# First token half of a fused attention and gated expert kernel in plain fp32 from unsplit weights

## The chip, the cores and the metric

One core of a Trainium2 chip runs the kernel. Its engines run side by side, each through its own queue in order: PE multiplies matrices, DVE (vector), ACT (scalar, with activation tables) and POOL work on tiles in the on-chip memory, and SP issues the transfers (DMA). The metric is the device time of one execution in microseconds (us), as a median over several executions.

## The reference

The attention looks at a window of 31 keys around each query and at one summary per block of 32 keys (the maximum of the keys, the mean of the values). Its output goes, heads side by side, into a gated expert layer in which each token is mixed with the one before it.

```python
scores_l = scale * np.matmul(q, k.transpose(0, 1, 3, 2))      # q, k, v: 4 x 8 x 768 x 64
scores_s = scale * np.einsum('bhsd,bhnd->bhsn', q, k_sum)
scores_s = scores_s + np.log(block)
scores_l_m = np.where(mask_l, scores_l, -1000000000.0)
scores_all = np.concatenate([scores_l_m, scores_s], axis=-1)
a = np.exp(scores_all - np.max(scores_all, axis=-1, keepdims=True))
a = a / (np.sum(a, axis=-1, keepdims=True) + 1e-09)
x = np.matmul(a, np.concatenate([v, v_sum], axis=2))
...
xk = mu_k * x + (1.0 - mu_k) * x_prev                         # 4 x 768 x 512
xr = mu_r * x + (1.0 - mu_r) * x_prev
k = np.maximum(xk @ w_k, 0.0)                                 # w_k 512 x 1024
v = k * k @ w_v                                               # w_v 1024 x 512
r = 1.0 / (1.0 + np.exp(-(xr @ w_r)))                         # w_r 512 x 512
return r * v
```

The queries, keys and values are fp32; the three weights arrive as fp64 and are turned into fp32 on the chip.

## The kernel before

**Units.** A batch has 8 heads in 4 pairs and 768 tokens in two halves of 384. A unit (`unit`) is one pair of heads for one half: on PE the scores (tile `sc`, 12 small matmuls), on DVE six masks with a row minimum (L439), on ACT six exponentials (L443), on DVE one inverse of the sums (L449, L450), on POOL six normalisations (L455), on PE six transposes (L462), on ACT two copies (L466), on PE the values (tile `av`, 12 small matmuls, L475), and a copy of the result into `vx` as features by tokens. `load_set` loads a pair's keys (`kt`) and value windows (two `vx`), makes the key maxima on DVE, and for batch 0 makes the value means on PE (L367, L387), which DVE or POOL spread into the windows (L393).

**Token halves.** The expert layer runs for eight halves, here n = 0 to 7 (n = 2 x batch + half). `mixes` makes the mixed tokens of four pairs: ACT or POOL scales (L498, L501), DVE adds (L504), ACT rounds to a high part (L507), DVE subtracts for a low part (L509). The parts have the type fp32r; each product of two numbers is made as high x high, high x low and low x high. The gate is 3 token tiles of 4 x 3 products of 512 columns (L521 to L523). `experts` then runs over 8 slices j of the hidden size: `first` (e1 in the texts, L542) has 12 products of 384 columns, then relu and square on ACT and a split into `kh` and `kl`; `second` (e2, L563) has 9 products of 512 columns. At the end DVE multiplies by the gate (L585) and SP stores.

**Weights.** There are 20 tiles of 128 x 512 (4 of w_r, 8 each of w_k and w_v). Each is loaded as 64-bit words into one of three slots `st`; ACT or POOL scales (L287, L290), DVE takes bits three times (L294, L297, L301) to give an fp32 tile, ACT or POOL rounds it to the high part (L309, L311) and DVE subtracts for the low part (L313). High and low parts of all 20 tiles have places of their own until the end.

**The order.** The code states operations with their costs and due times; `Plan.schedule` keeps a clock for each engine, takes for each engine the operation that can start first (then the one due first), hands out buffers from small pools, and writes the instructions in that order. The hardware keeps this order on each engine; what it waits for there is its own matter. At the start, matmuls on the identity (L618, "warm") fill PE until the first gate is issued. Before the change the order of the statements is: weights, all eight units of batch 0, gate of n = 0, gate of n = 1 between the slices of n = 0, and from there on each half's gate and experts with the next batch's units between.

```python
                    late = start > now
                    key = (start if late else now, o.due, o.n)
...
                for w, s in ((wk_h, 0), (wk_h, 1), (wk_l, 0)):
                    for p in range(NPAIR):
                        nc.tensor.matmul(ps.t[:, 0:HT], w[:, j, p, :], x[p][s].t, start=(n == 0), stop=(n == 11))
```

## Time and profile before

| what | value |
|---|---|
| median of 3 runs (475.34 to 480.13 us) | 479.1 us |
| span of the profiled execution | 476.2 us |
| median run less profiled span | 2.9 us |
| mean granted PE clock | 0.991 |
| memory traffic | 42.49 MB read, 6.29 MB written |
| DMA share of hardware queue | 36.0% of 16 engines' span |

No time of the profiled execution is recorded beside its span, and one of the three runs (475.34 us) is below that span, so executions differ by about that much.

In the page a row of a timeline reads: start, length, engine, line and operation, tile written and tiles read, shape, count, and in brackets how long the engine was idle before it and what ended that. The length of a row reaches past the start of the next row of its engine, so the cost of one instruction in a stream is the distance from its start to the next start. A matmul in plain fp32 leaves two records, so the 12 matmuls of a unit's scores or values show as x24. In the table by stretches, each engine has its busy time in the stretch and the number of instructions, then the granted PE clock, the busy share of the DMA engines and their GB/s.

### The profile page before, as it was taken

Reading aid. Unit: us, or ns where it says so; the run is one execution under the profiler, and the core shown is the slowest. Engines: PE = TensorE matmul, PEld = TensorE weight load, DVE = VectorE, ACT = ScalarE, POOL = GpSimd, SP = SyncE. Lnnn points to the kernel's source line nnn. Section 1 sums busy time; section 2 is a strip of 40 time slices with the busy share of each in tenths; the row PEclk is TensorE's granted clock in tenths of the full one; section 3 lists DMA queues with packets and bytes.
Section 4 is the critical chain, followed back from the end, with each engine's and each line's share of the span. In section 5 each row is a group of like instructions: output and inputs, shape, how many; then the busy total and the mean of one; then the engine's idle time right before and its main releaser. Section 6 shows DMA issues by size and latency. Waiting matters only on the chain.

```text
span 476.2 us, 9814 instructions
## 1 busy us (share of the span) xinstructions
PE 450.8 (95%) x3588; PEld 380.2 (80%) x3588; DVE 278.9 (59%) x881; ACT 285.9 (60%) x808; POOL 120.6 (25%) x255
## 2 busy tenths in 40 slices
PE   2899898879999999999999999999999999999996
PEld 2677776669888888987788888997778888888995
DVE  4699799979855386438364566429354554223223
ACT  3689675585777575428796756428886655231321
POOL 0579812230444301202342200203342201000000
PEclk9999999979999999999999999999999999999999
DMA  8991347885600209706300209907100010001001
GB/s 260 289 300 59 89 137 232 279 238 176 204 18 14 61 1 280 217 0 207 104 9 14 78 7 274 234 0 236 50 8 9 13 41 28 0 1 66 0 1 66
DMA packets 27014, 51.17 MB, mean 107 GB/s; under 512 B 2903, under 2 KB 14807, under 8 KB 26967
## 3 DMA queue, kind: packets, MB, share of 16 engines
q1 hardware_dynamic: 26967, 50.56, 36.0%
q8 instruction: 28, 0.46, 0.4%
q14 instruction: 19, 0.16, 0.1%
HBM read 42.49 MB, written 6.29 MB: 102 GB/s over the span
## 4 chain that ended last, share of the span: by engine, by line
PE 71%; ACT 8%; DVE 5%; POOL 3%; issue 2%; DVEq 0%; ACTq 0%; POOLq 0%
PE mm L563 26%; PE mm L542 25%; PE av L475 4%; PE pt L462 4%; PE mm L521 3%; PE mm L523 3%; PE mm L522 3%; PE sc L428 3%; POOL y L455 3%; ACT y L443 2%; ACT L443 2%; DVE we L297 1%; DVE xa L504 1%; DVE wc L301 1%; ACT xa L498 1%
## 5 line engine op out<-in xcount | busy, mean ns | idle before, releaser
L455 POOL TENSOR_SCALAR y<-y,rc 128x120 f32<-128x120 f32 x192 | 86.2, 467 | 164.2 <-DVE rc L450 140.1
L542 PE MATMUL mm<-xs,wk_h 128*128 128x384 f32 x512 | 102.3, 342 | 4.7 <-ACT z L527 4.1
L542 PEld LDWEIGHTS mm<-xs,wk_h 128*128 128x128 f32 x512 | 91.5, 190 | 11.0 <-ACT z L527 4.3
L547 ACT ACTIVATE r<-mm 128x384 f32<-128x384 f32 x64 | 31.3, 488 | 95.2 <-PE mm L542 95.0
L443 ACT ACTIVATE y<-y,mn 128x120 f32<-128x120 f32 x192 | 73.6, 386 | 11.1 <-DVE mn L439 10.1
L563 PE MATMUL mm<-wv_h,kh 128*128 128x512 f32 x192 | 78.7, 410 | 0.0
L563 PE MATMUL mm<-wv_l,kh 128*128 128x512 f32 x192 | 75.8, 395 | 0.0
L551 DVE CAST kh<-r 128x384 fp32r<-128x384 f32 x45 | 17.0, 378 | 73.8 <-ACT r L549 73.7
L563 PE MATMUL mm<-wv_h,kl 128*128 128x512 f32 x192 | 59.7, 406 | 0.0
L439 DVE CUSTOM_DVE_ANT_0 y<-sc,mask_sb 128x120 f32<-128x120 f32 x192 | 43.0, 276 | 24.6 <-PE sc L428 18.7
L542 PE MATMUL mm<-xs,wk_l 128*128 128x384 f32 x256 | 56.5, 343 | 0.0
L509 DVE TENSOR_TENSOR xs<-xa,xs 128x384 fp32r<-128x384 f32 x64 | 36.2, 575 | 25.1 <-ACT xs L507 25.0
L542 PEld LDWEIGHTS mm<-xs,wk_l 128*128 128x128 f32 x256 | 46.7, 192 | 0.0
L504 DVE SCALAR_TENSOR_TENSOR xa<-vx,mu_sb,xa 128x384 f32<-128x384 f32 x64 | 40.1, 646 | 6.4 <-ACT xa L498 3.8
L563 PEld LDWEIGHTS mm<-wv_h,kh 128*128 128x128 f32 x192 | 36.3, 189 | 7.1 <-issue 0.3
L553 DVE TENSOR_TENSOR kl<-r,kh 128x384 fp32r<-128x384 f32 x64 | 36.6, 571 | 7.9 <-ACT kh L552 5.1
L466 ACT COPY pts<-pt 120x384 f32<-120x384 f32 x64 | 30.4, 475 | 17.9 <-PE pt L462 17.5
L563 PEld LDWEIGHTS mm<-wv_l,kh 128*128 128x128 f32 x192 | 36.3, 189 | 5.8
L521 PE MATMUL mm<-wr_h,xs 128*128 128x512 f32 x96 | 38.8, 404 | 1.4 <-ACT r L547 1.3
L563 PEld LDWEIGHTS mm<-wv_h,kl 128*128 128x128 f32 x192 | 34.3, 188 | 6.9 <-DVE kl L553 0.2
L523 PE MATMUL mm<-wr_h,xs 128*128 128x512 f32 x96 | 38.4, 400 | 1.5 <-DVE xs L509 1.4
L462 PE MATMUL pt<-ident_sb,y 128*120 128x128 f32 x192 | 35.4, 288 | 3.6 <-POOL y L455 3.1
(63 smaller groups left out, 650.5 us busy)
## 6 DMA issues: line engine op xcount, KB each, us to landing
vx<-in_v SPq DMA_DIRECT2D x32, 360.0 KB
kt<-in_k SPq DMA_DIRECT2D x15, 544.0 KB
qt<-in_q SPq DMA_DIRECT2D x32, 192.0 KB
out<-z SPq DMA_DIRECT2D x24, 256.0 KB
st<-in_vT SPq DMA_DIRECT2D x12, 384.0 KB
st<-in_w_k SPq DMA_DIRECT2D x8, 512.0 KB
st<-in_w_v SPq DMA_DIRECT2D x8, 512.0 KB
st<-in_w_r SPq DMA_DIRECT2D x4, 512.0 KB
```

The lines of the kernel that those rows point to most:

```text
L439: op("DVE", "mask", None, lambda h=h, i=i, var=var: nc.vector.tensor_tensor_reduce(out=y[h].t[:, i, :], in0=sc[h].t[:, i, 0:NK], in1=mask_ ...
L443: op("ACT", "exp", None, lambda h=h, i=i: nc.scalar.activation(y[h].t[:, i, :], y[h].t[:, i, :], AF.Exp, bias=mn[h].t[:, i:i + 1], scale=-1.0,
L455: op("POOL", "norm", None, lambda h=h, i=i: nc.gpsimd.tensor_scalar(out=y[h].t[:, i, :], in0=y[h].t[:, i, :], scalar1=rc.t[:, NSL * h + i: ...
L462: nc.tensor.transpose(out=pt[h].t[0:NK, i * P:(i + 1) * P], in_=y[h].t[:, i, :], identity=ident_sb)
L504: op("DVE", "mixd", None, lambda xt=xt, xa=xa, p=p: nc.vector.scalar_tensor_tensor(out=xa.t, in0=xt.t[:, 1 + lo:1 + lo + HT], scalar=mu_sb ...
L509: op("DVE", "sub", None, lambda xa=xa, xh=xh, xl=xl: nc.vector.tensor_tensor(out=xl.t, in0=xa.t, in1=xh.t.bitcast(F32), op=ALU.subtract), ...
L521: nc.tensor.matmul(ps.t, xh.t[:, ts], wr_h[:, p, :], start=(p == 0), stop=False)
L523: nc.tensor.matmul(ps.t, xl.t[:, ts], wr_h[:, p, :], start=False, stop=(p == NPAIR - 1))
L542: nc.tensor.matmul(ps.t[:, 0:HT], w[:, j, p, :], x[p][s].t, start=(n == 0), stop=(n == 11))
L547: op("ACT", "relu", None, lambda: nc.scalar.activation(r.t, ps.t[:, 0:HT], AF.Relu), reads=[(ps, 0)], writes=[(r, 0)])
L553: op("DVE", "sub", None, lambda: nc.vector.tensor_tensor(out=kl.t, in0=r.t, in1=kh.t.bitcast(F32), op=ALU.subtract), reads=[(r, 0), (kh, 0 ...
L563: nc.tensor.matmul(acc[t].t, a.t[:, t * P:(t + 1) * P], w[:, j, :], start=start, stop=stop)
```

## The change

It does the following.

- The half n = 0 is computed in plain fp32. Its mixed tokens are not split (`mix` returns one tile), its gate has 12 matmuls of 512 columns (`gate_parts`), e1 has 4 matmuls of 384 columns per slice and e2 has 3 of 512, and the squared hidden tile `r` is used as it is. They read the fp32 weights before any split.
- The gate of n = 0 runs by pairs of heads: for each pair three matmuls, one for each token tile, as soon as that pair's tokens are mixed. Three accumulators stay open meanwhile.
- Only the four units of the first half of batch 0 stand ahead of n = 0; the other four are stated behind it with their own due times. A fourth `kt` place is needed for that; later it serves as two `z` tiles.
- `weight` ends with the fp32 tile. The split of all 20 tiles is a function of its own (`split`), stated behind n = 0. Fp32 tiles, high and low parts take their places from a common pool `w` of 40 slots, given back after the last use, instead of fixed places.
- The gate of n = 1 no longer stands between the slices of n = 0.
- The scheduler counts POOL's operations and those of DVE named in `LOCKS` as users of one port, one after the other; buffers can be taken out of turn; the planned DMA rate, due times and spacings are other numbers.

```diff
+GATE0 = 34000
+FULL = 34000
+STEP0 = 6800
+GATE1 = 92000
-GATES = (36000, 46000)
-WR = 0, 6000
+LOCKS = {"wbits", "wor", "wsub", "mixd", "sub", "kcopy", "khv", "spread"}
...
+                    if e == "POOL" and o.name != "tiny" or e == "DVE" and o.name in LOCKS:
+                        start = max(start, port)
...
-            if o.name == "gate" and spare:
+            if o.name == "gate32" and spare:
...
+    last_kt = Slot(const, "kt3", [P, KL], "kt3")
+    last_z = Slot(const, "z4", [P, 2, DM], "kt3")
     pools = dict(
+        ktx=[last_kt], w=slots("w", 2 * (NCK + 2 * NCV), [P, 512]),
...
-        z=tiles("z", 6, [P, DM]), xa=tiles("xa", 4, [P, HT]),
+        z=tiles("z", 4, [P, DM]), xa=tiles("xa", 4, [P, HT]),
...
-    def weight(name, i, src, dst_h, dst_l, due=None):
+    def weight(name, i, src, last, due=None):
         st, we, wc = buf("st"), buf("we"), buf("wc")
+        wf = w_f[name, i] = buf("wc") if last else buf("w", F32, False)
...
+    def split(name, i):
+        wf = w_f[name, i]
+        wh, wl = w_h[name, i], w_l[name, i] = buf("w", F32R, False), buf("w", F32R, False)
+        op("ACT", "wcast", None, lambda: nc.scalar.copy(out=wh.t, in_=value()), reads=[(wf, 0)], writes=[(wh, 0)],
...
+        op("DVE", "wsub", None, lambda: nc.vector.tensor_tensor(
+            out=wl.t, in0=value(), in1=wh.t.bitcast(F32), op=ALU.subtract), reads=[(wf, 0), (wh, 0)], writes=[(wl, 0)])
...
+    def mix(b, hf, which, p):
+        first = b + hf == 0
+        xt, xa = xts[b, p], buf("xs") if first else buf("xa")
...
+        if first:
+            return xa
...
+    def gate_parts(x, z):
+        ps = [buf("mm") for _ in range(NTT)]
+        for p in range(NPAIR):
+            for t in range(NTT):
+                op("PE", "gate32", GATE0 - (NPAIR - 1 - p) * FIRST + 930 * t, lambda p=p, t=t: nc.tensor.matmul(
+                    ps[t].t, x[p].t[:, t * P:(t + 1) * P], w_f["wr", p].t, start=(p == 0), stop=(p == NPAIR - 1)),
...
+                h, l = (w_f["wk", j], None) if single else (w_h["wk", j], w_l["wk", j])
+                terms = [(h, 0)] if single else [(h, 0), (h, 1), (l, 0)]
...
+                op("PE", "e2_32" if single else "e2a", due, high, reads=[(kh, 0), *w], writes=[(a, 0) for a in acc])
...
     for p in range(NPAIR):
-        e = load_set(0, p)
-        for h in range(2):
-            unit(0, p, h, e, GATES[0] - 2000 - (7 - 2 * p - h) * FIRST)
+        sets.append(load_set(0, p))
+        unit(0, p, 0, sets[p], GATE0 - 4000 - (NPAIR - 1 - p) * FIRST)
+        gates.append(mix(0, 0, 1, p))
+    z = [buf("z") for _ in range(NTT)]
+    gate_parts(gates, z)
+    x = mixes(0, 0, 0)
+    for p in range(NPAIR):
+        unit(0, p, 1, sets[p], gate_due(0, 1) - 9000 - (NPAIR - 1 - p) * SECOND)
+    experts(0, 0, x, z)
+    for i in range(NCK):
+        split("wr", i)
+    for j in range(NCV):
+        split("wk", j)
+        split("wv", j)
```

What the scheduler made of it is read from the order of the instructions. On PE, where the first gate stands, the order before has four last warm matmuls behind the values of the eighth unit, and then the gate's products by token tile; `wr_h`, `wr_l` are the parts of w_r, and `xs` the parts of the mixed tokens.

```order
L618 MATMUL mm_150<-ident_sb 128x128 x4
L521 MATMUL mm_153<-wr_h,xs_118 128x512
L522 MATMUL mm_153<-wr_l,xs_118 128x512
L523 MATMUL mm_153<-wr_h,xs_119 128x512
L521 MATMUL mm_153<-wr_h,xs_120 128x512
L522 MATMUL mm_153<-wr_l,xs_120 128x512
L523 MATMUL mm_153<-wr_h,xs_121 128x512
```

The same place on PE after the change shows the second and third pair's gate matmuls (L580, `w` is an fp32 tile of w_r) among a value mean (L425) and the transposes of the last pair's unit (L500).

```order
L580 MATMUL mm_135<-w_0_449,xs_0_416 128x512
L425 MATMUL mm_132<-sp_90,sel_sb 24x128
L580 MATMUL mm_133<-w_0_449,xs_0_416 128x512
L580 MATMUL mm_134<-w_0_449,xs_0_416 128x512
L580 MATMUL mm_135<-w_0_495,xs_0_489 128x512
L500 MATMUL pt_130<-ident_sb,y_93 120x128 x3
L580 MATMUL mm_133<-w_0_495,xs_0_489 128x512
L500 MATMUL pt_130<-ident_sb,y_94 120x128 x3
```

Gate matmuls of early pairs have moved ahead of the later pairs' transposes and values, and there are 15 warm matmuls in all where there were 56.

On DVE, ahead of the first gate, the order before mixes and splits the tokens (`xa` is mixed, `xs` its low part) between weights.

```order
L294 TENSOR_SCALAR we_143<-st_140 128x512
L504 SCALAR_TENSOR_TENSOR xa_117<-vx_79,mu_sb,xa_117 128x384
L504 SCALAR_TENSOR_TENSOR xa_114<-vx_70,mu_sb,xa_114 128x384
L504 SCALAR_TENSOR_TENSOR xa_115<-vx_73,mu_sb,xa_115 128x384
L509 TENSOR_TENSOR xs_125<-xa_117,xs_124 128x384
L504 SCALAR_TENSOR_TENSOR xa_116<-vx_76,mu_sb,xa_116 128x384
L509 TENSOR_TENSOR xs_127<-xa_114,xs_126 128x384
```

After the change DVE has at that place, ahead of the first e1, the last bits and splits of w_r (L328, L332, and L352 for the subtraction), those of the first tile of w_k, and then five mixes in a row, the last of the gate and the four for e1.

```order
L352 TENSOR_TENSOR w_0_516<-w_0_495,w_0_500 128x512
L328 SCALAR_TENSOR_TENSOR we_125<-st_122,we_125 128x512
L332 SCALAR_TENSOR_TENSOR w_0_524<-wc_127,we_125 128x512
L325 TENSOR_SCALAR we_125<-st_123 128x512
L328 SCALAR_TENSOR_TENSOR we_125<-st_123,we_125 128x512
L352 TENSOR_TENSOR w_0_559<-w_0_524,w_0_529 128x512
L332 SCALAR_TENSOR_TENSOR w_0_563<-wc_126,we_125 128x512
L541 SCALAR_TENSOR_TENSOR xs_0_561<-vx_79,mu_sb,xs_0_561 128x384
L541 SCALAR_TENSOR_TENSOR xs_0_565<-vx_70,mu_sb,xs_0_565 128x384
L541 SCALAR_TENSOR_TENSOR xs_0_567<-vx_73,mu_sb,xs_0_567 128x384
```

The subtractions of the tokens are gone there; those of the weights still stand among the bits. Of the 20 weight splits, the scheduler puts 4 subtractions on DVE ahead of the first e1, 12 between it and the last token split that the gate of n = 1 needs, and 4 behind.

More of the change, by code (lines that the diff above doesn't have):

```diff
@@ L185, in schedule @@
                 engines[e] = start + o.cost
+                if e == "POOL" and o.name != "tiny" or e == "DVE" and o.name in LOCKS:
+                    port = start + o.cost
                 o.finish = start + o.cost + TAIL[e]
@@ L199, in schedule @@
                         if not x.left:
[L200 removed]
+                            free_slots[x.pool].append((start, x.place))
                 spare = []
@@ L233, in tile_kernel @@
     )
-    plan = Plan(pools)
+    plan = Plan(pools, dict(ktx=("z", [Slot(const, "z", None, part=(last_z, n)) for n in range(2)])))
     op, buf = plan.op, plan.buf
@@ L241, in tile_kernel @@
     om_sb = const.tile([P, 2, NPAIR], F32, name="om_sb")
-    wk_h = const.tile([P, NCV, NCK, P], F32R, name="wk_h")
-    wk_l = const.tile([P, NCV, NCK, P], F32R, name="wk_l")
-    wv_h = const.tile([P, NCV, DM], F32R, name="wv_h")
-    wv_l = const.tile([P, NCV, DM], F32R, name="wv_l")
-    wr_h = const.tile([P, NCK, DM], F32R, name="wr_h")
-    wr_l = const.tile([P, NCK, DM], F32R, name="wr_l")
     pool_sb = const.tile([NK, 36], F32, name="pool_sb")
@@ L515, in gate_tile, with sigmoid @@
+    def mixes(b, hf, which):
+        return [mix(b, hf, which, p) for p in range(NPAIR)]
+    def sigmoid(ps, z):
+        op("ACT", "sigmoid", None, lambda: nc.scalar.activation(z.t, ps.t, AF.Sigmoid), reads=[(ps, 0)], writes=[(z, 0)])
     def gate_tile(b, hf, x, z, t):
@@ L525, in gate_tile @@
+                nc.tensor.matmul(ps.t, xl.t[:, ts], h, start=False, stop=(p == NPAIR - 1))
         op("PE", "gate", gate_due(b, hf) + 2800 * t, products, reads=[(a, 0) for pair in x for a in pair]
-           + [(("wr", i), s) for i in range(NCK) for s in "hl"], writes=[(ps, 0)])
-        op("ACT", "sigmoid", None, lambda: nc.scalar.activation(z[t].t, ps.t, AF.Sigmoid),
-           reads=[(ps, 0)], writes=[(z[t], 0)])
-    def experts(b, hf, x, z, between):
+           + [(w["wr", i], 0) for i in range(NCK) for w in (w_h, w_l)], writes=[(ps, 0)])
@@ L579, in last @@
                 def last(t=t):
[L580 to L584 removed]
+                    if single:
+                        product(t, kh, w_f, stop=True)
+                    else:
+                        product(t, kh, w_h)
+                        product(t, kh, w_l)
+                        product(t, kl, w_h, stop=True)
+                op("PE", "e2l_32" if single else "e2", due + 700 * t, last,
+                   reads=[(kh, 0), *([] if single else [(kl, 0)]), *w], writes=[(acc[t], 0)])
                 op("DVE", "result", due + 4000 + 700 * t, lambda t=t: nc.vector.tensor_tensor(
@@ L593, in experts @@
         for j in range(1, NCV + 1):
-            for work in between.get(j, ()):
-                work()
             if j < NCV:
@@ L600, in experts @@
             second(j - 1)
-    def places(name, i):
-        if name == "wr":
-            return wr_h[:, i, :], wr_l[:, i, :]
-        if name == "wv":
-            return wv_h[:, i, :], wv_l[:, i, :]
-        return [w[:, i].rearrange("p c n -> p (c n)") for w in (wk_h, wk_l)]
     for i in range(NCK):
-        weight("wr", i, w_r[i * P:(i + 1) * P, :], *places("wr", i), due=WR[0] + WR[1] * i)
+        weight("wr", i, w_r[i * P:(i + 1) * P, :], False)
     for j in range(NCV):
-        weight("wk", j, w_k[:, j * P:(j + 1) * P].rearrange("(c p) n -> p c n", p=P), *places("wk", j))
-        weight("wv", j, w_v[j * P:(j + 1) * P, :], *places("wv", j))
-    spare = buf("mm")
+        weight("wk", j, w_k[:, j * P:(j + 1) * P].rearrange("(c p) n -> p c n", p=P), False)
+        weight("wv", j, w_v[j * P:(j + 1) * P, :], j == NCV - 1)
+    spare = buf("mm", F32, False)
     for _ in range(WARM):
@@ L642, in tile_kernel @@
                     unit(b + 1, p, h, e, gate_due(b + 1, 0) - 14000 - (7 - 2 * p - h) * UNITS)
+        x, z = mixes(b, hf, 1), [buf("z") for _ in range(NTT)]
+        for t in range(NTT):
+            gate_tile(b, hf, x, z, t)
+        experts(b, hf, mixes(b, hf, 0), z)
     order = plan.schedule()
```

187 lines of the change are left out of this document (100 added, 87 removed).

## The prediction

> **What bounds the kernel now.** I read the page's head first, then the busy time by stretches, then PE's timeline and DVE's over the first 175 us.
>
> ```profile
> span 476.2 us, 9814 instructions
> PE 450.8 (95%) x3588; PEld 380.2 (80%) x3588; DVE 278.9 (59%) x881; ACT 285.9 (60%) x808; POOL 120.6 (25%) x255
> ```
>
> By this PE is the bound everywhere. The stretches (us; busy PE, PEld, DVE, ACT, POOL; granted clock; DMA share; GB/s) say otherwise for the first fifth.
>
> ```profile
> 20.00:30.00 10.00, 10.00 (x181) 7.99 (x180) 8.95 (x36) 8.61 (x35) 6.14 (x11) 1.00 1.02 263
> 40.00:50.00 10.00, 8.31 (x114) 6.72 (x113) 8.92 (x33) 7.99 (x33) 10.00 (x17) 1.00 0.27 69
> 60.00:70.00 10.00, 9.67 (x44) 7.59 (x42) 8.89 (x17) 7.58 (x14) 0.99 (x1) 1.00 0.36 118
> 80.00:90.00 10.00, 9.81 (x65) 7.81 (x64) 9.96 (x20) 5.65 (x10) 1.83 (x2) 1.00 0.81 263
> 100.00:120.00 20.00, 19.41 (x96) 17.03 (x99) 17.65 (x38) 12.64 (x30) 3.59 (x9) 0.86 0.57 174
> 200.00:300.00 100.00, 99.35 (x817) 84.18 (x816) 55.58 (x194) 66.56 (x191) 19.74 (x48) 1.00 0.32 89
> ```
>
> From 200 us on PE is full and DVE at 56%. Up to 90 us it is DVE that is full at about 90%. PE's timeline shows how little its busy time is worth there.
>
> ```profile
> 38.85 0.52 PE L462 MATMUL pt<-ident_sb,y 128*120 128x128 f32 x3
> 39.20 1.50 PE L618 MATMUL mm<-ident_sb 128*128 128x128 f32 x12
> ...
> 58.22 0.48 PE L521 MATMUL mm<-wr_h,xs 128*128 128x512 f32 x1
> 58.53 0.39 PE L522 MATMUL mm<-wr_l,xs 128*128 128x512 f32 x1
> 58.76 0.40 PE L523 MATMUL mm<-wr_h,xs 128*128 128x512 f32 x1
> 59.00 0.39 PE L521 MATMUL mm<-wr_h,xs 128*128 128x512 f32 x1
> ...
> 97.55 1.77 PE L542 MATMUL mm<-xs,wk_h 128*128 128x384 f32 x8 [3.88 <-ACT z L527]
> ...
> 173.75 0.40 PE L521 MATMUL mm<-wr_h,xs 128*128 128x512 f32 x1
> ```
>
> The first gate starts only at 58.22. The gate of n = 2 starts at 173.75, and 302.4 us follow to the end of the span; behind that gate both orders hold the same matmuls (216 of the gate, 576 of e1, 441 of e2, 16 units). So the change is worth what it does to these 173.75 us. The chain of waits gives prices where PE runs full.
>
> ```profile
> 111.93 2.08 PE mm L542 x12
> 114.01 2.09 PE mm L563 x9
> ...
> 123.41 0.78 PE sc L428 x24
> 124.19 0.85 PE av L475 x24
> ```
>
> **PE's work, added and moved.** A split product of 512 columns costs 0.2325 (59.00 less 58.53, halved), one of 384 costs 0.174 (2.08/12). For plain fp32 the warm row is the price: 12 records are 6 matmuls of 128 columns, with 0.11 between records, so 0.22 per 128 columns and 0.88 to 0.93 per 512; I take 0.93, four times 0.2325, and 0.70 for 384. Gate: 12 x 0.93 for 36 x 0.2325, +2.8. e1: 32 x 0.70 for 96 x 0.174, +5.7. e2: 24 x 0.93 for 72 x 0.2325, +5.6. Together +14.1 us of PE on n = 0 (at 0.88 it is +11.5). Forty-one fewer warm matmuls take off 9.0 us that were fillers, worth nothing where PE waits.
>
> Summed with these prices over the order after (0.78 a unit's scores, 0.85 its values, 0.34 three transposes), PE has 28.0 us ahead of the first e1, 53.5 from there to the gate of n = 1, and 58.2 from there to the gate of n = 2. Before, the 290.7 us behind the gate of n = 2 took 298.7 up to the last matmul, a pace of 1.027; so 53.5 and 58.2 take 54.9 and 59.8 if PE never waits.
>
> **DVE's work, removed and kept.** Spacings come from these rows.
>
> ```profile
> 19.29 0.55 DVE L393 COPY vx<-vm 24x768 f32<-24x768 f32 x1 [0.35 <-ACT vm L389]
> ...
> 20.08 0.28 DVE L439 CUSTOM_DVE_ANT_0 y<-sc,mask_sb 128x120 f32<-128x120 f32 x1
> ...
> 20.28 0.28 DVE L439 CUSTOM_DVE_ANT_0 y<-sc,mask_sb 128x120 f32<-128x120 f32 x1
> ...
> 41.10 1.35 DVE L504 SCALAR_TENSOR_TENSOR xa<-vx,mu_sb,xa 128x384 f32<-128x384 f32 x2
> ...
> 58.02 0.55 DVE L509 TENSOR_TENSOR xs<-xa,xs 128x384 fp32r<-128x384 f32 x1
> 58.49 0.61 DVE L504 SCALAR_TENSOR_TENSOR xa<-vx,mu_sb,xa 128x384 f32<-128x384 f32 x1
> 59.02 0.54 DVE L509 TENSOR_TENSOR xs<-xa,xs 128x384 fp32r<-128x384 f32 x1
> ...
> 62.01 0.55 DVE L509 TENSOR_TENSOR xs<-xa,xs 128x384 fp32r<-128x384 f32 x1
> ...
> 65.80 0.69 DVE L313 TENSOR_TENSOR wv_l<-wc,wv_h 128x512 fp32r<-128x512 f32 x1
> 66.40 0.85 DVE L294 TENSOR_SCALAR we<-st 128x512 uint32<-128x512 uint32 x1
> ...
> 69.28 0.43 DVE L294 TENSOR_SCALAR we<-st 128x512 uint32<-128x512 uint32 x1
> 69.62 0.55 DVE L509 TENSOR_TENSOR xs<-xa,xs 128x384 fp32r<-128x384 f32 x1
> 70.09 0.68 DVE L297 SCALAR_TENSOR_TENSOR we<-st,we 128x512 uint32<-128x512 uint32 x1
> 70.69 0.55 DVE L509 TENSOR_TENSOR xs<-xa,xs 128x384 fp32r<-128x384 f32 x1
> ...
> 75.20 0.54 DVE L553 TENSOR_TENSOR kl<-r,kh 128x384 fp32r<-128x384 f32 x1
> ...
> 90.61 0.54 DVE L553 TENSOR_TENSOR kl<-r,kh 128x384 fp32r<-128x384 f32 x1
> ...
> L585 DVE TENSOR_TENSOR z<-mm,z x24: 684/691/693, 122.4 to 472.5; 128x512 f32<-128x512 f32 x24
> ```
>
> A mask is 0.20, a mix 0.53, a token split 0.47, a weight's first bits 0.34, each later bit step 0.61, its split 0.60, a spread 0.55. The change removes 8 token subtractions, 8 of the hidden tile and its copies, some 8 to 10 us. It removes no weight work: by the order, 16 of 20 splits still stand on DVE ahead of the gate of n = 1. What it does is let PE begin n = 0 sooner.
>
> *To the first e1.* From the first spread (19.29 before; the bytes ahead of it and ahead of the last value window are the same in both orders, so I leave it) DVE has 22.2 us by these spacings to the last mix for e1: 9 masks, 6 spreads, 15 weight steps, 4 splits, 8 mixes, small rest. Before, from that spread to the mix at 41.10 stood 18.5 us of work in 21.8, a pace of 0.85. So 22.2/0.85 = 26.1, and the first e1 at 45.4 us. In PE's queue the last gate matmuls end there too: 28.0 us of work, of which some 15 lie behind the first gate matmul.
>
> *To the gate of n = 1.* DVE has 50.0 us between the last mix and the last token split: 36 masks (7.2), 42 weight steps (21.9), 12 splits (7.2), 10 mixes and token splits (5.1), small rest (8.6). Almost the same list stood before between 62.01 and the first result at 122.4: 50.8 us in 59.9 (from 62.48), pace 0.85. So 50.0/0.85 = 59.0, more than PE's 54.9: DVE decides, and the gate of n = 1 starts at 104.4.
>
> *To the gate of n = 2.* DVE has 30.3 us there, PE 59.8: PE decides, 164.2. Before it was 173.75.
>
> The gate by pairs adds a wait: PE's queue holds the third pair's gate matmuls ahead of the last pair's transposes, so a late mix of the third pair delays the last unit, and the three open accumulators leave one `mm` tile for the value means. Between nothing and the length of one pair's gate matmuls (3 x 0.93), I take nothing, since DVE, not PE, brings the last mix.
>
> ```profile
> L443 ACT ACT_TABLE_LOAD x9 | 11.5, 1283 | 0.9 <-PEq L726 0.7
> ```
>
> Costed at nothing, too: 4 more table loads on ACT (4 x 1.28 = 5.1 us) and 13 mixes that POOL did; ACT has room (5.65 to 8.61 of 10 in the stretches above), and without it those 5 us are due. SP's queue: the last w_v tile is its load 58, with 21 MB up to it, 81 us at the 263 GB/s of the stretch in which the DMA share is 1.02, while DVE gets to it after 100 us; if weights came late instead, DVE would wait, not SP. The fourth `kt` place becomes `z` after the last unit's scores, ahead of any use. The 40 shared slots: a split waits if its place's last reader is a late e1 (0 to 2 us, hidden by DVE's other work). The scheduler's port only spaces instructions.
>
> The sum: 164.2 + 302.4 = 466.6 us of span against 476.2, and with the 2.9 us of median over span, 469.5 us.
>
> **A rule against it.** POOL's normalisations slow down beside DVE.
>
> ```profile
> 50.53 4.50 POOL L455 TENSOR_SCALAR y<-y,rc 128x120 f32<-128x120 f32 x6
> ...
> 124.74 2.06 POOL L455 TENSOR_SCALAR y<-y,rc 128x120 f32<-128x120 f32 x6 [16.99 <-DVE rc L450]
> ```
>
> Six take 2.06 with a quiet DVE and 4.50 beside weight steps, so 2.44 us were lost; had all POOL work to be added to DVE's, the middle part would grow by up to 16.2 us, as the first rival works out. The Trainium skill (SBUF — State Buffer, section "SBUF: two separate sides") says that a DVE instruction with two inputs in the on-chip memory and a POOL instruction that reads there take one lock for their whole length, and that the later one waits until it is free. By that rule the time would be the 476.7 of the first rival; the trace agrees as far as the loss of 2.44 us goes.
>
> **The rivals.** *Full lock, no gain (0.22).* Between the first e1 and the gate of n = 1, POOL has 36 normalisations (36 x 0.343) and about 4 us of copies, 16.2 in all. If none of it overlaps DVE and DVE has no other idle time, the middle part is 66.2, the gate of n = 2 at 171.4, and the time 476.7. Against it: 15 of DVE's 50 us are masks and reductions, and the pace of 0.85 holds some blocking already.
>
> *The pace of the crowded start lasts, slower (0.11).* From 41.10 to 58.02 DVE did 11.6 us of work in 16.9, 0.69, since it waited for units that waited for POOL, which was busy 10.00 of 10.00. Half 1's units now stand among n = 0's slices. At 0.69 the whole 72.2 us of DVE take 104.6, the gate of n = 2 comes at 183.7, and the time is 489. The point that decides is 72.2/(173.75 - 59.8 - 19.3) = 0.76: below this pace the kernel is slower than before. An idle stretch of PE as at 97.55 (3.88 us, then the clock at 0.86 over 100 to 120) costs some 3 us more, and the warm matmuls that fill such gaps now end at the first gate.
>
> *PE bound from the first e1 on (0.17).* DVE at 0.94 (14.5 us of work between 75.20 and 90.61): 42.9 + 54.9 + 59.8 gives 157.6 and a time of 462.9.
>
> *Forecast (0.50).* The pace of 0.85 and 469.5 us.
>
> **How the numbers follow.** A median of this kernel can tell about 1% (4.8 us) from no change. Faster by over 1% means under 474.3, a pace over 0.80: the forecast and the PE-bound rival, 0.67. Within 1%: the lock rival, 0.22. Slower: 0.11. The range goes from 461 (PE-bound, with fp32 at 0.88 instead of 0.93) to 483 (pace 0.73), which leaves out most of the slow rival and a little below.
>
> **What would show it.** First e1 (L601 after) near 45 us; gate of n = 1 (L567) near 104; gate of n = 2 near 164, and the same 302 us behind it; fp32 records of 512 columns 0.46 apart; DVE near 90% busy from 25 to 100 us. It is wrong if PE waits for the hidden tile or the values rather than for DVE's weights, if normalisations take over 0.7 us throughout, or if the part behind the gate of n = 2 changes.

## The result and the profile after

The changed kernel takes 473.87 us (median of 4 runs, 471.08 to 475.29) against 477.92 us before (475.34 to 480.13): a ratio of 0.990 with a 95% interval from 0.9858 to 0.9943. The forecast was 469.5 us, its range 461 to 483. The sign was right and the range held; of the 9.6 us that the sum took off the span the medians show 4.05, under half. That is less than the 1% (4.8 us) that counted as measurable, though the interval does not reach 1; the median lies under the 474.3 us named there only because the kernel before was at 477.92 this time, not 479.1. The profiled execution of the changed kernel had a span of 473.5 us and a time of 475.29, so 1.8 us lie around a span. The 2.9 us that the forecast added were partly the difference between two executions.

The head of the page, then the stretches that were read before the change, with the one from 50 to 60 us added (us, busy PE, PEld, DVE, ACT, POOL, granted clock, DMA share, GB/s):

```profile
span 473.5 us, 9475 instructions
PE 447.6 (95%) x3438; PEld 357.9 (76%) x3438; DVE 267.0 (56%) x865; ACT 292.6 (62%) x815; POOL 112.5 (24%) x236
```

```profile
20.00:30.00 10.00, 10.00 (x161) 8.33 (x161) 7.86 (x33) 7.09 (x25) 4.03 (x9) 1.00 1.00 246
40.00:50.00 10.00, 8.53 (x69) 4.57 (x67) 9.79 (x28) 8.59 (x14) 0.84 (x1) 1.00 0.40 126
50.00:60.00 10.00, 6.56 (x57) 4.09 (x57) 5.94 (x27) 9.90 (x30) 4.83 (x8) 0.75 0.45 134
60.00:70.00 10.00, 10.00 (x50) 5.34 (x49) 8.78 (x24) 8.43 (x28) 8.03 (x12) 0.91 0.58 195
80.00:90.00 10.00, 10.00 (x98) 5.93 (x97) 9.96 (x41) 8.80 (x34) 3.86 (x7) 1.00 1.03 307
100.00:120.00 20.00, 17.41 (x139) 11.96 (x134) 17.68 (x54) 16.80 (x43) 7.93 (x15) 1.00 0.69 183
200.00:300.00 100.00, 99.27 (x814) 83.69 (x813) 54.77 (x193) 68.60 (x196) 23.02 (x52) 1.00 0.33 97
```

DVE is at 9.79 of 10 from 40 to 50 us and at 9.96 from 80 to 90, near the forecast's 90% and more. Between, from 50 to 60 us, lies a hole: DVE is at 5.94 there and ACT at 9.90: an engine that the forecast had called roomy is full there. PE's timeline shows the places that the forecast named.

```profile
44.77 2.84 PE L580 MATMUL mm<-w,xs 128*128 128x512 f32 x6 [1.47 <-DVE xs L541]
47.45 2.74 PE L601 MATMUL mm<-xs,w 128*128 128x384 f32 x8
50.12 0.84 PE L466 MATMUL sc<-kt,qt 64*64 64x120 f32 x24
53.95 0.33 PE L500 MATMUL pt<-ident_sb,y 128*120 128x128 f32 x1 [2.98 <-POOL y L493]
...
57.10 5.17 PE L601 MATMUL mm<-xs,w 128*128 128x384 f32 x8
...
109.34 0.50 PE L567 MATMUL mm<-w,xs 128*128 128x512 f32 x1 [0.79 <-ACT r L608]
...
124.72 0.52 PE L500 MATMUL pt<-ident_sb,y 128*120 128x128 f32 x3 [1.68 <-POOL y L493]
...
171.94 0.39 PE L567 MATMUL mm<-w,xs 128*128 128x512 f32 x1
```

Four fp32 matmuls of 384 columns take 50.12 - 47.45 = 2.67 us, so the price of plain fp32 (2.8 forecast) was nearly right. The sum goes wrong elsewhere: the first e1 comes at 47.45 (45.4 forecast), the gate of n = 1 61.9 us later (59.0), the gate of n = 2 62.6 us after that (59.8), and 301.6 us follow (302.4). 2.05 + 2.9 + 2.8 - 0.8 is the 6.9 us between the forecast span of 466.6 and 473.5.

PE's wait at 53.95 is for POOL's normalisations, which wait for DVE's inverse, which waits for ACT. ACT's timeline tells why.

```profile
46.20 0.61 ACT L349 CAST w<-w 128x512 fp32r<-128x512 f32 x1
46.83 1.28 ACT L558 ACT_TABLE_LOAD   x1
48.12 0.60 ACT L558 ACTIVATE z<-mm 128x512 f32<-128x512 f32 x1
48.74 1.28 ACT L481 ACT_TABLE_LOAD   x1
50.03 0.40 ACT L481 ACTIVATE y<-y,mn 128x120 f32<-128x120 f32 x1
...
52.43 1.28 ACT L558 ACT_TABLE_LOAD   x1
53.72 1.08 ACT L558 ACTIVATE z<-mm 128x512 f32<-128x512 f32 x2
...
56.33 1.28 ACT L481 ACT_TABLE_LOAD   x1
57.62 0.40 ACT L481 ACTIVATE y<-y,mn 128x120 f32<-128x120 f32 x1
```

The scheduler sets the first sigmoid (L558) ahead of the six exponentials (L481) of the unit that PE needs next, and the other two sigmoids behind them. It knows the length of each function, not that a switch between the two costs a table load. So those exponentials stand behind a load, a sigmoid and a second load, 3.2 us in all, and the next unit's behind two loads more. And PE, which paused for 2.98 us, then runs at half clock (the granted clock is the figure behind the five engines):

```profile
55.00:61.00 6.00, 5.99 (x32) 3.70 (x32) 3.06 (x18) 5.94 (x19) 2.23 (x5) 0.50 0.55 153
62.00:64.00 2.00, 2.00 (x8) 1.09 (x7) 2.00 (x9) 2.00 (x7) 2.00 (x4) 1.00 0.01 4
```

In all, the changed kernel has 22 loads where 18 stood before. The loads are shown by which function they were for (busy us and ns of one; idle before):

```profile
L481 ACT ACT_TABLE_LOAD x11 | 14.1, 1283 | 0.9 <-PEq L792 0.7
L558 ACT ACT_TABLE_LOAD x11 | 14.1, 1283 | 0.2
```

### The profile page after: what moved, and what is told of

It reads as the page before. It is cut to its first block, busy times and chain, and to the rows that moved or that the text cites. A ratio compares the mean times of both kernels' runs of the same rounds, so it can differ in the third digit from the quotient of the medians.

```text
span 473.5 us, 9475 instructions
## 1 busy us (share of the span) xinstructions
PE 447.6 (95%) x3438; PEld 357.9 (76%) x3438; DVE 267.0 (56%) x865; ACT 292.6 (62%) x815; POOL 112.5 (24%) x236
## 4 chain that ended last, share of the span: by engine, by line
PE 67%; ACT 12%; DVE 8%; DMA 8%; issue 2%; POOL 1%; SPq 1%; ACTq 0%; POOLq 0%; DVEq 0%
PE mm L627 23%; PE mm L601 22%; ACT y L481 5%; PE pt L500 4%; PE av L513 4%; DMA kt<-in_k 3%; PE mm L567 3%; PE mm L569 3%; PE mm L568 3%; PE sc L466 2%; DMA pool_sb<-in_pool 2%; PE mm L580 2%; ACT L481 2%; DMA st<-in_w_k 1%; POOL y L493 1%
## 5 line engine op out<-in xcount | busy, mean ns | idle before, releaser
L601 PE MATMUL mm<-xs,w 128*128 128x384 f32 x736 | 152.1, 355 | 0.6 <-DVE w L332 0.6
L601 PEld LDWEIGHTS mm<-xs,w 128*128 128x128 f32 x736 | 131.3, 190 | 13.9 <-issue 3.7
L627 PE MATMUL mm<-w,kh 128*128 128x512 f32 x336 | 91.9, 402 | 0.0
L481 ACT ACTIVATE y<-y,mn 128x120 f32<-128x120 f32 x192 | 73.5, 386 | 10.7 <-DVE mn L477 10.4
L627 PEld LDWEIGHTS mm<-w,kh 128*128 128x128 f32 x336 | 60.7, 188 | 11.1 <-DVE kl L616 0.2
L627 PE MATMUL mm<-w,kl 128*128 128x512 f32 x168 | 52.4, 407 | 0.1
L500 PE MATMUL pt<-ident_sb,y 128*120 128x128 f32 x192 | 33.9, 285 | 6.4 <-POOL y L493 6.0
L466 PE MATMUL sc<-kt,qt 64*64 64x120 f32 x768 | 30.4, 289 | 8.6 <-DMA pool_sb<-in_pool 6.8
L500 PEld LDWEIGHTS pt<-ident_sb,y 128*120 128x120 f32 x192 | 22.8, 139 | 19.0 <-POOL y L493 9.6
L481 ACT ACTIVATION_READ_ACCUMULATOR y<-y,mn 128x1 f32 x192 | 36.3, 189 | 0.0
L627 PEld LDWEIGHTS mm<-w,kl 128*128 128x128 f32 x168 | 30.0, 188 | 6.5 <-DVE kl L616 0.5
L567 PE MATMUL mm<-w,xs 128*128 128x512 f32 x84 | 33.6, 400 | 1.1 <-ACT r L608 0.8
L610 ACT ACTIVATE r<-r 128x384 f32<-128x384 f32 x64 | 33.6, 525 | 1.2
```

Of the source, the lines that this page charges most:

```text
L466: nc.tensor.matmul(sc[h].t[cs, i, 0:NK], qt.t[hs, n * QW:(n + 1) * QW], kt.t[hs, w * KB:w * KB + NK], start=True, stop=True,)
L481: op("ACT", "exp", None, lambda h=h, i=i: nc.scalar.activation(y[h].t[:, i, :], y[h].t[:, i, :], AF.Exp, bias=mn[h].t[:, i:i + 1], scale=-1.0,
L500: nc.tensor.transpose(out=pt[h].t[0:NK, i * P:(i + 1) * P], in_=y[h].t[:, i, :], identity=ident_sb)
L567: nc.tensor.matmul(ps.t, xh.t[:, ts], h, start=(p == 0), stop=False)
L601: nc.tensor.matmul(ps.t[:, 0:HT], w.t[:, p * P:(p + 1) * P], (x[p] if single else x[p][s]).t, start=(n == 0), stop=(n == len(terms) * NPAI ...
L610: op("ACT", "square", None, lambda: nc.scalar.activation(r.t, r.t, AF.Square), reads=[(r, 0)], writes=[(r, 0)])
```

## The experiments

The theory after the profile was that these loads, costed at nothing, ate the missing gain. The rivals were that DVE's work alone sets the pace, that the half clock is the cost, and (for the first e1) that the gate by pairs holds up the last unit. Each kernel below is the changed one but for its edit, except where it says otherwise. This table has for each profiled execution the first e1, the lengths of the three parts behind it as far as the gate of n = 1, the gate of n = 2 and the end of the span (us, from the first records of those matmuls), and the median with its ratio to the kernel before on the same chip. The kernels ran on several chips, on which the median of the kernel before went from 477.2 to 478.9 us, so medians of different rows that lie within 1 to 2 us are not told apart; and each length is that of one execution.

| kernel | first e1 | to gate n = 1 | to gate n = 2 | to the end | median | ratio, 95% interval |
|---|---|---|---|---|---|---|
| before | | (173.75 in all) | | 302.4 | 477.92 | |
| changed | 47.45 | 61.9 | 62.6 | 301.6 | 473.87 | 0.990 (0.986 to 0.994) |
| tanh in both places | 46.28 | 58.3 | 60.1 | 300.5 | 466.99 | 0.978 (0.974 to 0.981) |
| before, with tanh | | (167.87 in all) | | 300.1 | 470.39 | 0.986 (0.982 to 0.990) |
| one sigmoid moved | 46.66 | 59.1 | 62.6 | 301.2 | 471.46 | 0.987 (0.983 to 0.991) |
| warm matmuls in the pause | 46.93 | 62.3 | 62.6 | 301.2 | 474.56 | 0.994 (0.991 to 0.997) |
| tanh, PE light | 48.53 | 54.6 | 62.1 | 299.2 | 466.13, one run | |
| tanh, DVE light | 46.34 | 53.8 | 60.1 | 299.3 | 461.42, one run | |
| no port | 47.13 | 62.4 | 63.7 | 302.0 | 477.46 | 1.000 (0.998 to 1.002) |
| tanh, no port | 46.96 | 61.4 | 60.4 | 299.7 | 470.56 | 0.982 (0.978 to 0.985) |
| tanh, pairs late, second edit | 47.13 | 60.0 | 60.1 | 299.1 | 467.21 | 0.978 (0.975 to 0.982) |
| tanh for n = 0 only | 45.48 | 61.5 | 62.6 | 301.1 | 472.5 | 0.991 (0.988 to 0.995) |
| tanh, warm matmuls | 45.19 | 57.6 | 60.2 | 299.1 | 466.84 | 0.978 (0.974 to 0.983) |

### No table switches

```diff
-        op("ACT", "sigmoid", None, lambda: nc.scalar.activation(z.t, ps.t, AF.Sigmoid), ...
+        op("ACT", "sigmoid", None, lambda: nc.scalar.activation(z.t, ps.t, AF.Tanh, scale=0.5), ...
-            op("ACT", "square", None, lambda: nc.scalar.activation(r.t, r.t, AF.Square), ...
+            op("ACT", "square", None, lambda: nc.scalar.activation(r.t, r.t, AF.Square, scale=0.7071067811865476), ...
-                op("DVE", "result", ..., lambda t=t: nc.vector.tensor_tensor(
-                    out=z[t].t, in0=acc[t].t, in1=z[t].t, op=ALU.mult), ...
+                op("DVE", "result", ..., lambda t=t: nc.vector.scalar_tensor_tensor(
+                    out=z[t].t, in0=z[t].t, scalar=1.0, in1=acc[t].t, op0=ALU.add, op1=ALU.mult), ...
```

> The changed kernel with its 22 table loads cut to 1: the sigmoid is formed as (1 + tanh(x/2))/2, tanh being found in the same table as exp, the 1 added in the result's multiplication and the 1/2 put into the square of the hidden tile. No instruction changes its place. Theory (ACT's table loads at the first e1 held up the softmax of the unit and so PE and its clock): the 2.98 us of waiting at PE's first transposes behind the first e1 fall under 1 us, the half clock from 55 us on is gone, the gate of n = 1 starts at 101 to 105 us instead of 109.3, that of n = 2 at 163 to 168 instead of 171.9, and the kernel takes 464 to 470 us. Rival (DVE's work sets the pace of this stretch, the loads are only seen beside it): the gate of n = 1 moves by less than 1.5 us and the time stays within 2 us of the changed kernel's 473.9.

It takes 466.99 us, 6.9 less than the changed kernel. The wait at the transposes fell to 1.20 us (under 1 was expected), and the wait of 1.68 us at 124.72 is gone:

```profile
50.99 0.33 PE L500 MATMUL pt<-ident_sb,y 128*120 128x128 f32 x1 [1.20 <-POOL y L493]
...
104.62 0.50 PE L567 MATMUL mm<-w,xs 128*128 128x512 f32 x1 [0.72 <-ACT r L608]
...
164.76 0.39 PE L567 MATMUL mm<-w,xs 128*128 128x512 f32 x1
```

The two parts behind the first e1 now take 58.3 and 60.1 us, within 0.7 us of the forecast's 59.0 and 59.8; for the first of them this is in part luck, as the next section works out. The half clock is not gone, only half as long:

```profile
54.00:57.00 3.00, 3.00 (x6) 1.50 (x5) 2.97 (x12) 2.74 (x12) 1.66 (x3) 0.50 0.36 114
58.00:60.00 2.00, 2.00 (x8) 1.09 (x7) 1.63 (x8) 1.45 (x5) 0.65 (x2) 1.00 0.10 35
```

The Trainium skill (ScalarE: Activation LUTs, section "Table sets: the hidden batching unit") says that exp and tanh lie in one set and calls for grouping by set; the trace agrees, with one load instead of 22.

The same edit in the kernel before:

> The kernel before with the same edit, 18 table loads cut to 1. If the loads are a cost that the change brought, by setting exps of half 1 among the first sigmoids, the kernel before gains little from it: the wait of 3.88 us at its first e1 (for the first sigmoid's result) loses one or two loads, 1.3 to 2.6 us, and with it the half clock behind it can go, 2 to 3 us more; 473 to 478 us, so a smaller gain than the changed kernel has. If the loads cost the same in both (rival), both kernels gain the same within 1 us and the ratio between them stays 0.99.

The rival holds: 470.39 us, 7.5 less than before, so the loads cost the kernel before as much as the changed one. The wait of 3.88 us, which the expectation puts at the first e1 and the first sigmoid, stands in fact at an e1 at 97.55, long behind the first e1 (66.69), and is for the sixth sigmoid, the last of n = 1. It fell to 0.98, the half clock that followed it is gone, and the gate of n = 2 comes at 167.87 instead of 173.75.

```profile
93.77 1.66 PE L542 MATMUL mm<-xs,wk_h 128*128 128x384 f32 x8 [0.98 <-ACT z L527]
...
167.87 0.40 PE L521 MATMUL mm<-wr_h,xs 128*128 128x512 f32 x1
```

```profile
97.00:106.00 9.00, 8.70 (x43) 7.79 (x44) 8.96 (x20) 6.51 (x15) 5.17 (x7) 1.00 0.80 222
```

So the change is worth 470.39 - 466.99 = 3.4 us without loads and 4.05 with them. The loads do not explain why the change brings little, since it brings no more without them; how they bear on the forecast the next section works out.

### One sigmoid moved

```diff
     order = plan.schedule()
+    sig = [o for o in order if o.name == "sigmoid"]
+    order.remove(sig[0])
+    order.insert(order.index(sig[1]), sig[0])
```

> The changed kernel with one instruction moved: the first sigmoid of n = 0 is issued right ahead of the second, behind the six exps of the unit that PE waits for, so two of the 22 table loads go and the exps start some 3.2 us sooner (two loads and a sigmoid). Theory: PE's 2.98 us in front of the transposes go and with them the half clock, 4 to 6 us off the gate of n = 1 (103 to 105.5 us) and 468 to 470.5 us in all. Rival (DVE's pace): under 1.5 us off the gate of n = 1, and 472 to 475 us.

Two loads less and one instruction moved give 471.46 us. The part up to the gate of n = 1 loses 2.8 us; the next part keeps its 62.6, since the loads of n = 1 are still there. DVE's wait for ACT's softmax in the first of these parts, 5.4 us in the changed kernel, is 2.8 here. The gain is below the 4 to 6 us of the theory and above the rival's bound. The half clock stayed, for 6.8 us (a loss of 3.4) as in the changed kernel, though PE's pause at the transposes had shrunk to 1.2 us; whether it is what held the gain down is not shown. The pause of 2.98 us is not what the half clock needs.

### Warm matmuls in the pause

```diff
+    at = next(i for i, o in enumerate(order) if o.name == "e1_32")
+    at = next(i for i, o in enumerate(order) if i > at and o.name == "transpose")
+    def fill():
+        for _ in range(12):
+            nc.tensor.matmul(pools["av"][0][:, 0:P], ident_sb, ident_sb, start=True, stop=True)
...
+    order.insert(at, extra)
```

> The changed kernel with 12 warm matmuls of 128 columns (2.6 us) ahead of the transposes that PE waits 2.98 us for, all else in its place. It takes no wait away, only PE's pause. If the half clock of 6.8 us behind that pause is what costs, it goes and some 3 us with it (gate of n = 1 at 106 to 107 us, 470 to 471.5 us in all). If the loss is the late softmax itself, or DVE's pace, the gate of n = 1 stays at 109 us within 1 us and the time within 1.5 us of 473.9.

The clock is whole (1.00 in every stretch) and nothing is gained: 474.56 us, 62.3 us up to the gate of n = 1. So with the loads in place the half clock costs nothing that shows; DVE waits for ACT's softmax meanwhile, 6.1 us in that part, and 1.7 us for keys from the DMA.

### PE light and DVE light

In the first of these, three of four pairs' products in the gate and in e1 of n = 0 and six of eight slices of its e2 are left out; in the second, the sign bit of each weight. Both have tanh.

```diff
-                op("PE", "gate32", ..., lambda p=p, t=t: nc.tensor.matmul(..., start=(p == 0), stop=(p == NPAIR - 1)), ...
+                op("PE", "gate32", ..., lambda p=p, t=t: p == NPAIR - 1 and nc.tensor.matmul(..., start=True, stop=True), ...
+                        if not single or p == NPAIR - 1:
...
+                            if j == 0:
                                 product(t, kh, w_f, start=True)
```

> The changed kernel without table switches (tanh, as before), and with most of PE's work on n = 0 left out: of the first gate and of its e1 only the last pair's products, of its e2 only slices 0 and 7. Between the first e1 and the gate of n = 1 PE's 53.5 us of work become 20. If DVE's weight work decides that stretch (the forecast's view), it stays at 56 to 59 us (58.3 with all products). If PE decides it now that the loads are gone, it falls under 50 us.

```diff
-        op("DVE", "wor", None, sign, ...
+        op("DVE", "wor", None, lambda: None, ...
```

> The changed kernel without table switches (tanh), and with one of DVE's three steps of each weight left out (the sign bit: 20 steps of 0.61 us, 5 of them ahead of the first e1 and 14 behind it up to the gate of n = 1), so the weights lose their signs. If DVE decides, the first e1 comes 3 us sooner (43 us) and the stretch to the gate of n = 1 shrinks from 58.3 us to what PE needs, 54 to 55.5. If PE decides that stretch, it stays within 1 us of 58.3; if the first e1 waits for units and not for DVE, it stays at 46 us.

With 33.5 us of PE's 53.5 gone, the part up to the gate of n = 1 lost only 3.7 us and stayed at 54.6 (at a mean clock of 0.69), between the two expectations; with 8.5 us of DVE's gone it lost 4.5 and came to 53.8, just under PE's own 54.9, at a whole clock (1.00 for 0.97). These rows hold exactly that part for the changed kernel, for tanh, and for the two light ones (columns as above):

```profile
47.45:109.34 61.89, 55.61 (x379) 31.22 (x377) 54.35 (x168) 51.89 (x149) 26.63 (x45) 0.94 0.76 226
...
46.28:104.62 58.34, 54.04 (x379) 30.12 (x377) 54.40 (x168) 46.62 (x144) 26.26 (x45) 0.97 0.81 241
...
48.53:103.11 54.58, 33.95 (x294) 20.26 (x293) 51.81 (x159) 43.58 (x132) 27.01 (x45) 0.69 0.87 256
...
46.34:100.14 53.80, 52.23 (x378) 29.37 (x376) 45.80 (x154) 46.20 (x145) 24.96 (x45) 1.00 0.86 260
```

DVE's busy time is the same 54.4 us with and without loads; what differs is its idle time, 7.5 us in the changed kernel and 3.9 with tanh. Its longest waits in that part (us in total, times, longest), first of the changed kernel, then with tanh:

```profile
DVE sm L487 <- ACT y L481: 5.4, 3, 2.6
...
DVE sm L487 <- ACT y L481: 1.5, 2, 0.9
```

So DVE decides this part, as forecast: it is busy 51.81 of 54.58 us with PE light, and PE, at 52.23 of 53.80 us with DVE light, stands only a little behind it. The first e1 did not move with DVE's work (46.34 for 46.28), where 3 us had been expected. DVE then waits for ACT right ahead of the mixes, for a rounded weight and a scaled token:

```profile
41.13 0.69 DVE L352 TENSOR_TENSOR w<-w,w 128x512 fp32r<-128x512 f32 x1 [1.12 <-ACT w L349]
...
42.99 2.74 DVE L541 SCALAR_TENSOR_TENSOR xs<-vx,mu_sb,xs 128x384 f32<-128x384 f32 x5 [0.56 <-ACT xs L535]
```

### The last unit and the gate by pairs

```diff
+    gate = [o for o in order if o.name == "gate32"]
+    turn = next(o for o in order[order.index(gate[6]):] if o.name == "transpose")
+    order.remove(turn)
+    order.insert(order.index(gate[6]), turn)
...
+    for o in gate[7:9]:
+        order.remove(o)
+    n = order.index(scores) + 1
+    order[n:n] = gate[7:9]
```

> Again the gate by pairs out of the last unit's way, without table switches (tanh): the last unit's first three transposes one gate matmul sooner, behind all three normalisations that they read, and the last two gate matmuls of the third pair behind the unit's values and the next scores. By the changed kernel's rows (normalisations that end at 38.0 us, a copy of 0.48 between the two groups of transposes) the values start 1 us sooner and PE's wait of 1.47 us goes. If PE's queue sets the first e1, it comes at 45.3 to 45.6 us instead of 46.3; otherwise it stays. If DVE's weight work binds behind it, the time stays at 467 us within 1; if the stretch just starts sooner, 466 us.

The values of the last unit did start sooner (39.60 instead of 40.44 us, though the normalisations ahead of them began 0.9 us later in this execution). But DVE's mix came no sooner, and the first e1 stayed, at 47.13, as late as the normalisations; the time is the same 467 us.

```profile
39.60 0.33 PE L513 MATMUL av<-pts,vx 120*64 120x64 f32 x2
40.24 0.91 PE L513 MATMUL av<-pts,vx 120*64 120x64 f32 x22 [0.31 <-ACT pts L504]
...
44.46 2.84 PE L580 MATMUL mm<-w,xs 128*128 128x512 f32 x6 [0.61 <-DVE xs L541]
47.13 2.74 PE L601 MATMUL mm<-xs,w 128*128 128x384 f32 x8
```

An edit before it had put the transposes one gate matmul further ahead, ahead of the last of the three normalisations that they read, so one of three blocks of one head in that unit went on unnormalised.

> The changed kernel without table switches (tanh), and with the gate by pairs taken out of the last unit's way in PE's queue: its first three transposes are issued two gate matmuls sooner, and the last two gate matmuls of the third pair come behind the unit's values and the next scores. If PE's queue, with gate matmuls of the third pair ahead of the last unit's transposes (the wait that the forecast put at nothing), sets the first e1, that e1 comes 1 to 1.8 us sooner (44.5 to 45.3 us, from 46.3). Whether the end follows shows what binds behind it: with DVE full from 40 us on by its weight work, the gate of n = 1 moves by less than 0.5 us and the time stays at 467 within 1 us; if the stretch simply starts sooner, 465.2 to 466 us.

Its first e1 came at 48.48 us, behind 3.4 us at half clock, and its 465.43 us are those of another computation; it says nothing about the question.

### The shared port

```diff
-                    if e == "POOL" and o.name != "tiny" or e == "DVE" and o.name in LOCKS:
-                        start = max(start, port)
```

> The changed kernel with the shared port taken out of the scheduler's start times, which then sets some 60 of DVE's instructions elsewhere; on the chip nothing else differs but two table loads fewer (20 for 22). If the port's spacing is worth something, by keeping POOL's normalisations and DVE's weight steps apart, their mean rises over 0.51 us and the time to 475 us or more. If it only shifts the plan, the time stays within 1.5 us of 473.9, or gains the 1 to 3 us that two loads less are worth.

> The plan made without the shared port once more, without table switches. The port's removal cost the changed kernel 3.6 us (477.5 for 473.9) while the normalisations kept their mean (497 ns for 507). If that cost was the places that the plan gave to exps and sigmoids, so table loads at worse points, it is gone here: 466 to 468.5 us, as with the port. If the order of DVE's and POOL's work itself is worse, 469.5 to 472 us.

Without the port's two lines the changed kernel takes 477.46 us, 3.6 more, and is as slow as the kernel before. Without loads it takes 470.56, again 3.6 more than its counterpart, but on another chip, and the intervals of the two ratios overlap there. So the cost does not look like a matter of the loads, nor is it one of slower normalisations (497 ns each for 507, 491 for 497 with tanh). These are the rows of the part up to the gate of n = 1, with loads and with tanh:

```profile
47.13:109.54 62.41, 56.75 (x402) 31.58 (x401) 58.98 (x176) 44.15 (x137) 32.64 (x52) 0.95 0.68 207
...
46.96:108.31 61.35, 55.78 (x403) 30.74 (x401) 58.62 (x176) 41.94 (x134) 33.06 (x52) 0.97 0.70 211
```

DVE has 176 instructions and 59.0 us there instead of 168 and 54.4. Without the port the plan gives ACT less (137 for 149 instructions) and DVE and POOL more. With tanh the part is 3.0 us longer for it (61.4 for 58.3), nearly the whole loss. With loads it is only 0.5 us longer (62.4 for 61.9), since DVE idles less there (3.4 us for 7.5), and the next part 1.1; the profiled executions are 1.7 us apart in all, so where the rest of the 3.6 lies is not shown.

### Tanh for n = 0 only, and warm matmuls with tanh

```diff
+           nc.scalar.activation(z.t, ps.t, AF.Tanh, scale=0.5) if first else
             nc.scalar.activation(z.t, ps.t, AF.Sigmoid), ...
```

> The changed kernel with tanh for n = 0 only (three sigmoids of 24), so 18 table loads of 22 stay, the four around the first e1 being gone. If the loads cost where PE waits for a softmax, and each place by itself, the stretch from the first e1 to the gate of n = 1 takes 58 to 59.5 us (61.9 with loads, 58.3 without any), the next one up to the gate of n = 2 stays at 62 to 62.6 (60.1 without any), and the time is 468.5 to 470.5 us. If the loads cost through ACT's total, the gain is spread and the first stretch gains under 1.5 us.

The second part stayed at 62.6 us, as expected. The first took 61.5 us, not 58 to 59.5, and the time is 472.5, above the expectation. Up to the gate of n = 1 this kernel issues the same instructions as the one with tanh everywhere, with no load among them, so its loss there comes from something else. DVE's wait for ACT's softmax is down to 1.8 us (5.4 with loads, 1.5 with tanh everywhere); in its place came 6.8 us at half clock instead of 3.4, with DVE waiting 2.8 us for PE's scores and transposes, and 1.8 us for keys from the DMA. So executions of the same instructions can differ by 3 us in this part, as much as the loads were held to cost there. The two rows show the clock.

```profile
45.48:106.95 61.47, 55.55 (x378) 31.15 (x376) 54.53 (x168) 46.51 (x144) 26.55 (x45) 0.94 0.76 229
...
45.19:102.76 57.57, 54.38 (x391) 30.87 (x389) 53.98 (x168) 46.62 (x144) 27.56 (x45) 1.00 0.81 239
```

The second row is the last experiment, 6 warm matmuls in the remaining pause of the kernel with tanh:

> The changed kernel without table switches (tanh), and 6 warm matmuls of 128 columns (1.3 us) where PE then still waits 1.20 us for the unit's normalisations. With the loads, filling PE's pause kept the clock whole and gained nothing, since DVE waited for ACT's softmax (5.4 to 6.1 us in this stretch). Without them DVE waits 1.5 us for ACT and 1.3 us for PE. If the clock's loss (half speed for 3.4 us, so 1.7 us) now lies on the path, by the scores and transposes that DVE waits for, it goes: 465.3 to 466.3 us and a stretch of 56.5 to 57.5 us from the first e1 to the gate of n = 1. If DVE's own work is all that counts, 467 us within 0.7 and 58 us as before.

In the profiled execution the clock was whole and the part took 57.6 us, the least of all with full work, and its 463.84 us were its fastest run. Over six runs (463.84 to 470.14) the median is 466.84, no different from 466.99. Within these six the time goes with the mean granted clock: three at 0.998 or more took 463.84 to 466.22 us, three at 0.996 or less 467.47 to 470.14. So the clock's loss seems to lie on the path once the loads are gone. But the six matmuls do not keep the clock whole in each execution, and the kernel without them had a run at 1.000 that took 467.39; whether filling this pause gains anything over many runs stays open.

## Why the prediction was right or wrong

**The failing step is the table loads.** "Costed at nothing, too: 4 more table loads on ACT ... ACT has room" took ACT's room from averages over 10 us. The loads cost not by their sum but by where they stand: ahead of the exponentials on which the chain to DVE's inverse, POOL's normalisations and PE's transposes hangs. For the part up to the gate of n = 2 this is clear: four kernels with the loads of n = 1 in place took 62.6 us, four without any 60.1 or 60.2, with 59.8 forecast. For the part up to the gate of n = 1 it is clear of DVE's wait for the softmax, 5.4 and 6.1 us with the four loads, 2.8 with two fewer, 0.8 to 1.8 with none. The length of that part went from 61.9 and 62.3 to 59.1 and then 58.3, but also to 61.5 and 60.0 without loads, where a half clock of 6.8 us stood; so how much of the 2.9 us by which the part was missed is due to the loads stays open.

**The pace of 0.85 was right by luck.** It was taken from the kernel before over a stretch in which three loads stand (93.03 to 98.03). With tanh, DVE has the same 123 instructions from the last token split to the first result in 54.2 us instead of 59.9. These are the rows of that stretch, before and before with tanh:

```profile
62.48:122.41 59.93, 52.35 (x271) 42.73 (x270) 54.36 (x123) 39.20 (x81) 12.70 (x19) 0.94 0.70 215
...
62.41:116.58 54.17, 49.45 (x273) 40.32 (x271) 53.39 (x123) 34.35 (x77) 14.62 (x19) 1.00 0.78 237
```

By the forecast's 50.8 us of work that is a pace of 0.94. In the changed kernel 50.0 us of work took 61.9 with loads, a pace of 0.81, and 58.3 without, 0.86. So a pace that the old order's loads had lowered met a new order that runs slower than the old one even without loads. At 0.94 the term would have been 53 us, below PE's 54.9, and PE would have been forecast to decide. DVE idles 3.9 us in the new order where it idled 0.8 in the old, both with tanh, and POOL is busy 26.3 us there instead of 14.6; what of this makes the difference is not shown.

**Why the gain was forecast too large.** The 59.8 us up to the gate of n = 2 assume that PE never waits, so no load costs anything there, and the sum came out at 164.2, where the changed kernel without loads stands (164.76). It was set against a measured kernel that has them: the wait of 3.88 us for a sigmoid and the half clock behind it stood in the 173.75 us. Without loads on both sides the gates of n = 2 stand at 167.87 and 164.76, 3.1 us apart; with loads on both sides at 173.75 and 171.94, 1.8 apart. The 9.6 us mixed the two.

**The first e1.** 45.4 us were forecast by DVE's weight work at a pace of 0.85. In six kernels that are alike up to there it came between 45.19 and 47.45, 46.3 in the mean, so the term was some 0.9 us short, and the rest is what one execution differs from another by. The reason given was right only in part. DVE, busy 9.66 of 10 us from 30 to 40 us, does bring the last mix, and a shorter way through PE's queue did not move it; but with 3 us less of DVE's work it did not move either, since DVE then waited for ACT. Each was tried in one execution, where alike kernels differ by up to 2.3 us. The wait put at nothing (the third pair's gate matmuls ahead of the last unit) does delay the values, by 0.8 us or more, but that alone decides nothing.

**DVE decides up to the gate of n = 1, PE up to the gate of n = 2.** Right: the first by the light kernels, with PE close behind; the second by the 60.1 or 60.2 us that four kernels with tanh show alike, whatever came before, PE being busy all of it. With PE light it was 62.1 us, at a clock of 0.96. With loads PE waited there (60.60 busy of 62.60 us).

**Plain fp32, the 302 us behind, the weights' arrival.** Right or nearly: 2.67 us (2.8 forecast) for four matmuls of 384 columns, 301.6 us, and DVE at 9.96 of 10 from 80 to 90 us, not waiting for weights.

**The port "only spaces instructions".** Right for the chip's instructions, but not for the value of the plan: the two lines decide which engine gets some of the work, and the plan without them takes 3.6 us more, nearly all that the change gains.

**The rivals.** The full lock (66.2 us in the middle, 476.7) did not come: the normalisations slowed to 507 ns from 467, and the middle was 61.9. The rule of the Trainium skill weighed beside it (SBUF — State Buffer, section "SBUF: two separate sides") would have given 476.7; the trace agrees with some loss, six normalisations taking 5.40 us beside a full DVE, and not with that sum.

```profile
33.80 5.40 POOL L493 TENSOR_SCALAR y<-y,rc 128x120 f32<-128x120 f32 x6 [0.42 <-DVE rc L488]
```

The slow pace of 0.69 did not come: it was 0.81. Its end note, an idle PE and then a half clock, did come, but cost nothing that shows while ACT was the later one. PE bound from the first e1 on came nearest with the loads gone and the clock whole (57.6 us for 54.9).

## What to carry to other kernels

Where a scheduler interleaves two activation functions from different tables, give the switch a price in the plan, or pick a function from the same table; the edit to tanh was worth some 1.5% here in either kernel, the restructuring 1.0%, and both together give 466.99 us, 2.2% under the kernel before (1.9 to 2.6). Before summing a gain, ask which stalls of the old trace the new sum leaves out silently, and price them in both; a pace taken over an old stretch has its stalls in it. When an engine that is "60% busy" feeds a chain, look at what stands ahead of that chain's instructions in its queue, not at its average.
